# An mLSTM layer with a fused expert block: q and k transposed on the host, scores and state in float32, the output gate in the normaliser

## The chip, the cores and the metric

The kernel runs on one core of one Trainium2 chip. A core has TensorE (matrix products into PSUM), VectorE (DVE), ScalarE (ACT), GpSimd (POOL), and SyncE (SP), which here issues all transfers. The metric is the device time of one launch in microseconds. Three timed runs of the kernel before gave 370.81, 371.1 and 376.52 us; the median is 371.1 us. The change is judged by the same median.

## The reference

For 4 sequences of 768 steps, 8 heads of 40 entries, a gated recurrence gives a row per step; the rows of the heads, side by side, are 3072 rows of 320, and these go through a two-layer block whose middle is a softmax times its own argument, normalised.

```python
m_new = np.maximum(f_gate[:, :, t] + m, i_gate[:, :, t])
f_stab = np.exp(f_gate[:, :, t] + m - m_new)
i_stab = np.exp(i_gate[:, :, t] - m_new)
C = f_stab * C + i_stab * np.einsum('bhd,bhe->bhde', vt, kt)
n = f_stab * n + i_stab * kt
y[:, :, t] = sigmoid(o_gate) * (C q) / np.maximum(np.abs(n q), 1.0)
# then, for all rows x of y:
h = x @ w_in                                   # 320 -> 1024
solu = h * softmax(h)
ln = (solu - mean) / np.sqrt(var + 1e-06) * g_ln
out = ln @ w_out                               # 1024 -> 320
```

The two weights come as float64.

## The kernel before, in words

The 768 steps are cut into 6 chunks of 128, and a *unit* is one chunk of one sequence: 24 units, chunk by chunk, the four sequences in turn. Inside a chunk the recurrence becomes matrix products. A scan over the gates (once, at the start) gives for each step two numbers, kept in `bG`: b, and the exponential of G, the decay since the chunk began. A unit is then:

- Loads: `tk` (v with a column of ones, q and k, row by row), `gb` (G broadcast to all partitions), and every fourth unit `sg` (the output gate for four units, made a sigmoid by ScalarE, L895).
- q and k: the largest entry of each row (`am`, L805), a scale (L819, L824), two float16 parts of each scaled row (`qs`: high parts by ScalarE L828, low parts by VectorE L836), and one transposing transfer to `qT` (L852). In `qT` the 40 entries of a head stand three times, so that one product with 120 rows has high x high, low x high and high x low.
- Decays: GpSimd masks `gb` (L867), ScalarE takes 8 exponentials (`d`, L882). k times the last column of d is `kt` (GpSimd, L904).
- Scores `ps` (8 float16 products, L924); VectorE multiplies them by the decays and the row scale into `p` (L936, two halves).
- y: TensorE multiplies p with v (`sy`, L982, 8 float32 products with 41 columns) and, from the second chunk on, q with the state before (L959, 16 products: the state has three bfloat16 parts, `cs`). VectorE scales the second by exp G (L967), adds the first (L989), and makes the normaliser from column 40 (`rd`: L999, L1008, L1014); x = y times it (L1019), and GpSimd multiplies by the gate (L1031).
- State: 8 products with `kt` as weights (L1045), GpSimd's decay (L1052), VectorE's sum (L1062), and its three bfloat16 parts (L1067, L1071, L1075, L1079), copied to other partitions by two transfers (L1083, L1084).
- x is transposed by TensorE (L1093) and cut into two parts (L1098 to L1110). First product `ph`: 16 products of 512 columns (L1139), in four groups.
- Middle: maximum (L1154), exponential (L1161), e = argument times exponential with its sum (L1169), squares about the mean (L1178). VectorE's small lines L1190 to L1212 collect variance and eps, GpSimd takes powers (L1221), L1229 and L1235 make `so`, the scale of the output rows. GpSimd centres and scales e (`uc`, L1246), ScalarE and GpSimd cut it into two float16 parts (`us`, L1265, L1251), and one transposing transfer gives `big` (L1256).
- Second product `so_`: 24 float16 products of 320 columns (L1283) with two parts of w_out; ScalarE scales them into `ot` (L1299), and a transfer stores them.

At the start the float64 weights are rebuilt as float32 by integer operations on VectorE (L514, L529, L539) and split into parts.

The order of the work is not written by hand. `Plan` records each group with a cost in ns, its reads and writes, and a preference from the table `RANK` (a unit's number plus the entry). `run()` goes through planned time, always gives each engine the best of what it takes to be ready, and issues the groups in that order; each engine keeps it. Groups of TensorE with a `mix` (in the kernel before p times v, and the second product) are issued matrix by matrix in turn where both are ready. Between `bG` and the scale of w_out, `fill` puts products of the identity (L1317) where TensorE would be idle in the plan. PSUM has eight banks: before, `ps` 2, `ph` 2, `sy` 2, `sx` 1 (update of the state, transposes of x), `so_` 1.

Of the kernel before, what the change touches and what calls it, by code (L numbers as in the profile page):

```python
# [20 lines left out]
L = 128  # L21
# [6 lines left out]
HE = H * E1  # L28
NEG = -1.0e30
# [4 lines left out]
SQ = 2.0**8  # L34
SU = 2.0**9
SW = 2.0**14


# var is kept as DFF var, and as var / (DFF SU)^2
EPS_Z = (1.0e-6 * DFF) ** 0.5  # L40
SU_C = 1.0 / (DFF * (DFF * SU) ** 2)

# PSUM buffers: scores, first product, y, small ones, second product
PSB, PHB = 2, 1
BIG = 5
SMALL = {"sy": 2, "sx": 1, "so_": 1}
# [3 lines left out]
RANK = {  # L50
    "sp tk": (12.09, -9.79, -11.5),
    "sp gb": (-1.49, 8.66, 14.2),
    "sp sg": (15.0, -7.54, 1.93),
    "act sg": (-7.1, -1.77, -13.37),
    "dve am": (11.86, -15.0, -0.91),
    "dve rr": (-11.16, -14.0, 13.87),
    "act qs": (0.45, 10.07, 9.68),
    "dve qs": (7.26, 7.15, 10.59),
    "sp qT": (-6.45, 5.48, 11.64),
    "act dec": (-9.23, 5.75, 11.77),  # L60
    "pool gb": (9.8, 13.99, -3.85),
    "act d": (5.39, -8.2, 3.61),
    "pool kt": (8.7, 3.48, -11.6),
    "pe ps": (-9.38, -8.42, 13.4),
    "dve p": (5.27, -1.43, -1.2),
    "pe sy": (0.12, 7.6, -4.18),
    "dve y": (-0.58, -12.54, 10.43),
    "dve rd": (-7.3, -14.52, 10.96),
    "dve x": (-15.0, -11.15, -2.45),
    "pool x": (-5.09, 5.53, 5.17),  # L70
    "pe sx": (-9.5, 2.25, 13.96),
    "pool cn": (8.92, 2.91, 1.53),
    "dve cn": (-2.98, -11.95, -10.92),
# [40 lines left out]
class Plan:  # L114
    """Orders instructions by their costs before any is issued.
# [1247 lines left out]
```

## Time and profile before

| | kernel before |
|---|---|
| timed runs | 370.81, 371.1, 376.52 us, median 371.1 |
| profiled execution, first to last instruction | 374.5 us |
| busy: TensorE, VectorE, ScalarE, GpSimd | 305.6, 323.4, 234.6, 241.9 us |
| mean granted TensorE clock | 0.917 |
| transfers on the hardware queue, share of 16 engines | 73.5% |

The profiled execution is another one than the three timed; its own time is not listed, only its span, so what is worked out from the profile is held against the span and then moved by the 3.4 us between span and median. "Busy" counts the time from an instruction's start to its end, with any wait for a port inside it; "idle before" is time in which an engine had nothing to do, and names what ended it.

### The profile page before, as it was taken

To read this page: it belongs to the slowest core of one execution; us is meant where nothing else is said; L and a number is where in the kernel's file an instruction comes from. 1 tells how busy PE (TensorE), PEld (TensorE's weight loads), DVE (VectorE), ACT (ScalarE), POOL (GpSimd) and SP (SyncE) were. 2 spreads that over 40 slices of the span, in tenths; PEclk is the share of its full clock that TensorE was granted. 3 is DMA by queue.
4 is the path that set the end of the run, shared out by engine and by line. 5 is a ranking of instruction groups with operands and counts; after the bars stand their busy time and mean duration, and the time that the engine had idled before them with its cause. 6 is when DMAs were issued, how large, how long until landed. Compare 5 with 4: busy or idle time off the path is not lost.

```text
span 374.5 us, 7096 instructions
## 1 busy us (share of the span) xinstructions
PE 305.6 (82%) x2469; PEld 251.2 (67%) x2469; DVE 323.4 (86%) x674; ACT 234.6 (63%) x489; POOL 241.9 (65%) x238
## 2 busy tenths in 40 slices
PE   0397969965999797789688885889969899999885
PEld 0397967954788576658566673678748687887653
DVE  8969896989999899999999999889998989865430
ACT  2437743959666667768687664839539879655531
POOL 5476493758696766779864895954866746746500
PEclk9999896988758899989999996969969989999999
DMA  7597989323797969789988897486889867373352
GB/s 224 160 255 219 289 207 279 111 57 96 158 219 193 190 161 184 162 187 235 197 175 153 217 243 164 143 177 136 245 188 205 192 186 166 76 155 74 76 137 63
DMA packets 118724, 65.09 MB, mean 174 GB/s; under 512 B 102880, under 2 KB 110816, under 8 KB 118688
## 3 DMA queue, kind: packets, MB, share of 16 engines
q1 hardware_dynamic: 118688, 64.64, 73.5%
q8 instruction: 19, 0.31, 0.3%
q14 instruction: 17, 0.14, 0.1%
HBM read 33.85 MB, written 4.03 MB: 101 GB/s over the span
## 4 chain that ended last, share of the span: by engine, by line
DVE 49%; PE 37%; issue 6%; DMA 3%; ACT 2%; POOL 1%; SPq 0%; DVEq 0%; ACTq 0%; POOLq 0%
PE ph L1139 14%; DVE qs L836 8%; PE sy L982 4%; DVE p L936 4%; DVE e L1169 4%; DVE nm L1154 4%; DVE so L1229 3%; DMA qT<-qs 3%; DVE am L805 3%; PE sx L1045 2%; DVE rd L1008 2%; DVE so L1235 2%; DVE cs L1075 2%; DVE x L1019 2%; DVE cs L1067 1%
## 5 line engine op out<-in xcount | busy, mean ns | idle before, releaser
L1283 PEld LDWEIGHTS <-big 128*128 128x128 f16 x576 | 64.7, 120 | 22.0 <-issue 6.6
L982 PEld LDWEIGHTS sy<-tk,p 128*128 128x128 f32 x384 | 60.9, 211 | 10.8 <-DVE p L936 8.0
L882 ACT ACTIVATE d<-gb,bG 128x128 f32<-128x128 f32 x192 | 60.0, 390 | 12.0 <-POOL gb L867 12.0
L982 PE MATMUL sy<-tk,p 128*128 128x41 f32 x384 | 59.7, 268 | 7.3 <-DVE p L936 7.3
L1251 POOL TENSOR_TENSOR us<-uc,us 128x1024 f16<-128x1024 f32 x23 | 49.9, 2170 | 14.7 <-ACT us L1265 14.7
L828 ACT ACTIVATE qs<-tk,rr 128x640 f16<-128x640 f32 x48 | 37.8, 822 | 21.1 <-DVE rr L824 15.1
L836 DVE SCALAR_TENSOR_TENSOR qs<-tk,rr,qs 128x320 f16<-128x320 f32 x48 | 44.4, 937 | 0.0
L1139 PE MATMUL ph<-wih,xh 128*128 128x512 f32 x96 | 37.0, 470 | 9.0 <-DVE e L1169 7.8
L1154 DVE TENSOR_REDUCE nm<-ph 128x1 f32<-128x1024 f32 x24 | 29.1, 1215 | 13.5 <-PE ph L1139 13.5
L1161 ACT ACTIVATE e<-ph,nm 128x1024 f32<-128x1024 f32 x24 | 26.6, 1110 | 22.4 <-DVE nm L1154 22.2
L936 DVE SCALAR_TENSOR_TENSOR p<-ps,am,d 128x512 f32<-128x512 f32 x48 | 34.7, 734 | 4.0 <-ACT d L882 2.7
L1178 ACT ACTIVATE sq<-e,nmean 128x1024 bf16<-128x1024 f32 x24 | 27.5, 1144 | 12.3 <-DVE e L1169 12.2
L1031 POOL TENSOR_TENSOR x<-x,sg 128x320 f32<-128x320 f32 x24 | 21.4, 892 | 18.8 <-DVE x L1019 12.4
L1045 PE MATMUL sx<-tk,kt 128*40 128x41 f32 x320 | 18.1, 217 | 18.1 <-DVE x L1110 16.9
L1139 PE MATMUL ph<-wil,xh 128*128 128x512 f32 x96 | 32.6, 423 | 0.0
L1265 ACT CAST us<-uc 128x1024 f16<-128x1024 f32 x24 | 24.9, 1038 | 11.3 <-POOL uc L1246 11.3
L1317 PE MATMUL so__188<-ident 128*128 128x128 f32 x206 | 30.0, 305 | 2.3 <-DVE bG L447 2.3
L1079 POOL TENSOR_TENSOR c<-cr,cs 40x328 bf16<-40x328 f32 x20 | 19.2, 960 | 19.6 <-DVE cs L1075 15.8
L1045 PEld LDWEIGHTS sx<-tk,kt 128*40 128x40 f32 x320 | 15.9, 131 | 22.5 <-issue 20.9
L1317 PEld LDWEIGHTS so__188<-ident 128*128 128x128 f32 x206 | 28.1, 218 | 2.7 <-DVE bG L447 2.5
L1221 POOL TENSOR_TENSOR pw<-ab,mhalf 128x2 f32<-128x2 f32 x24 | 17.3, 719 | 19.2 <-DVE ab L1212 14.7
L1139 PE MATMUL ph<-wih,xl 128*128 128x512 f32 x96 | 29.1, 429 | 0.0
(184 smaller groups left out, 811.0 us busy)
## 6 DMA issues: line engine op xcount, KB each, us to landing
gb<-gd SPq DMA_DIRECT2D x24, 512.0 KB
tk<-in_tok_dram SPq DMA_DIRECT2D x24, 484.0 KB
sg<-in_og_dram SPq DMA_DIRECT2D x12, 320.0 KB
out_dram<-ot SPq DMA_DIRECT2D x24, 160.0 KB
big<-in_w_out_dram SPq DMA_DIRECT2D x4, 640.0 KB
big<-in_w_in_dram SPq DMA_DIRECT2D x4, 512.0 KB
cs<-cs SPq DMA_DIRECT2D x20, 51.2 KB
cs<-c SPq DMA_DIRECT2D x20, 25.6 KB
```

Source lines behind the costliest of these rows:

```text
L828: nc.scalar.activation(out=q_dst(P, a)[:, :, s0 : s1 + 1 : s1 - s0, :], in_=q_src(P, a).unsqueeze(2).to_broadcast([L, H, 2, D]), func=AF.Copy,
L836: V.scalar_tensor_tensor(out=q_dst(P, a)[:, :, 1 + a, :], in0=q_src(P, a), scalar=P[rr][:, a : a + 1], in1=q_dst(P, a)[:, :, 0, :], op0=AL ...
L882: nc.scalar.activation(out=P[d_t][:, h, :], in_=P[gb][:, h, :], func=AF.Exp, bias=P[BG][:, 0, c, b * H + h : b * H + h + 1],)
L936: lambda P, j=j, ps=ps: V.scalar_tensor_tensor(out=P[p_t][:, 4 * j : 4 * j + 4, :], in0=P[ps], scalar=P[am][:, 1:2], in1=P[d_t][:, 4 * j : ...
L982: nc.tensor.matmul(o[:, h, :], lhsT=P[p_t][:, h, :], rhs=v1(P)[:, h, :], start=True, stop=True)
L1045: nc.tensor.matmul(o[:, h, :], lhsT=P[kt][:, h, :], rhs=v1(P)[:, h, :], start=True, stop=True)
L1139: nc.tensor.matmul(P[ph][:, j * 512 : (j + 1) * 512], lhsT=a, rhs=w[:, j * 512 : (j + 1) * 512], start=n == 0, stop=n == 7,)
L1154: lambda P: V.tensor_reduce(out=P[nm], in_=P[ph], axis=AX.X, op=ALU.max, negate=True),
L1178: lambda P: nc.scalar.activation(out=P[sq], in_=P[e], func=AF.Square, bias=P[nmean], scale=-float(DFF), accum_out=P[su]),
L1251: (V if last else nc.gpsimd).tensor_tensor(out=P[us[1]][:, 1], in0=P[uc], in1=P[us[0]][:, 0], op=ALU.subtract)
L1283: nc.tensor.matmul(P[po][:, 0:DM], lhsT=uTv(P, a)[:, k, :], rhs=P[w][:, k, :], start=n == 0, stop=n == 23)
L1317: nc.tensor.matmul(P[("so_", "idle")][:, 0:L], lhsT=P[I], rhs=P[I], start=True, stop=True)
```

## The change

What it does, part by part. Line numbers of the changed kernel's rows are its own.

- **q and k** come from the host transposed (`qkT`): for each unit a tile `qk` of 128 partitions, where the even heads of four pairs lie on partitions 0 to 39 and the odd ones on 64 to 103, zeros elsewhere. `tk` keeps v, the ones and k. Row maxima, scales, float16 parts and their transposing transfer are gone.
- **Scores** are 8 float32 products with 40 rows, a pair's two in turn on the lower and upper rows, into two banks.
- **State** is one float32 tile per sequence, `C`, with the two heads of a pair on the two halves of the partitions; update and use are 4 products each with 82 columns. Its bfloat16 parts and copies are gone. The chunk's decay comes from a small product at the start (`DEC`).
- **y** is summed in PSUM: q times state is scaled by exp G in place, and p times v is added by TensorE on top.
- **Gate**: ScalarE takes exp(-o) in place of the sigmoid; VectorE multiplies 1 + that by the normaliser, takes one reciprocal of 128x320 and multiplies y by it. GpSimd's product with the gate is gone.
- **w_out** is centred once (its column mean, times g, is subtracted), so e goes to float16 as it is, scaled by the row's maximum; GpSimd's `uc` is gone. The scale `so` is made from operations with one tensor operand.
- **PSUM**: `sy` has three banks for scores (two), y, update and transposes of x, taken in a fixed order (`place`); `ph` 2 x 2, `so_` 1.
- **Plan**: groups may carry `lock`; a VectorE group with it and any GpSimd group do not overlap in planned time. An order of issue alone (`issue`) no longer counts as a wait for the end. Costs and the table are new, and the state's two product groups have a `mix` too.
- Some of the start moves: two gate subtractions from GpSimd to VectorE, casts of w_in and the first step of w_out from GpSimd to ScalarE.

Where the order moves, at three places. First TensorE up to its first first product (`so__188`, `so__170`: the filler; `sx`, `sy` with x: transposes of x). Before:

```order
L982 MATMUL sy<-tk,p 128x41 x4
L1317 MATMUL so__188<-ident 128x128 x6
L1093 MATMUL sx<-ident,x 128x128 x2
L1093 MATMUL sx<-ident,x 64x128
L1317 MATMUL so__188<-ident 128x128 x3
L1139 MATMUL ph<-wih,xh 128x512 x2
L1139 MATMUL ph<-wil,xh 128x512 x2
```

On TensorE at the same place, now:

```order
L985 MATMUL sy<-tk,p 128x41 x4
L1051 MATMUL sy<-tk,kt_104 128x82 x4
L1306 MATMUL so__170<-ident 128x128 x15
L1092 MATMUL sy<-ident,x 128x128 x2
L1092 MATMUL sy<-ident,x 64x128
L918 MATMUL sy<-qk 128x128 x8
L1306 MATMUL so__170<-ident 128x128 x2
L1138 MATMUL ph<-wih,xh 128x512 x2
L1138 MATMUL ph<-wil,xh 128x512 x2
```

The next unit's scores now stand ahead of the first product, and those are the last fillers; before, 53 of 103 came after it.

Second, TensorE in a late unit of the changed kernel (`ph` first product, `qk` scores, `big` second product, `C` state):

```order
L1138 MATMUL ph<-wih,xl 128x512 x4
L1092 MATMUL sy<-ident,x 128x128 x2
L1092 MATMUL sy<-ident,x 64x128
L918 MATMUL sy<-qk 128x128 x8
L1138 MATMUL ph<-wih,x_2215 128x512 x2
L1138 MATMUL ph<-wil,x_2215 128x512 x2
L1271 LDWEIGHTS big
L1271 MATMUL so__2377<-woh,big 128x320
L958 MATMUL sy<-C_1243,qk 128x82
L1271 LDWEIGHTS big
L1271 MATMUL so__2377<-wol,big 128x320
L958 MATMUL sy<-C_1243,qk 128x82
```

Before, the 16 products of a unit with the state stood together; now its 4 stand between second products of another unit, and scores stand inside the first product.

Third, VectorE in the middle of the run (`nm` maximum, `qs` float16 parts, `cn` state, `e` the softmax product). Before:

```order
L1154 TENSOR_REDUCE nm<-ph 128x1
L967 TENSOR_TENSOR y<-sy,bG 128x328
L1229 SCALAR_TENSOR_TENSOR so<-ab,pw 128x1
L836 SCALAR_TENSOR_TENSOR qs_86<-tk,rr,qs_86 128x8x40
L1062 TENSOR_TENSOR cn_2210<-cn_2210,sx 40x328
L1235 TENSOR_TENSOR so<-so,ow 128x1
L836 SCALAR_TENSOR_TENSOR qs_86<-tk,rr,qs_86 128x8x40
L1190 TENSOR_SCALAR z<-z 128x1
L1169 SCALAR_TENSOR_TENSOR e,nmean<-ph,e 128x1024
```

On VectorE now, from the maximum to the same product:

```order
L1153 TENSOR_REDUCE nm<-ph 128x1
L931 TENSOR_TENSOR p<-sy,d 128x512
L971 TENSOR_TENSOR sy<-sy,bG 128x328
L1167 TENSOR_SCALAR mx<-nm 128x1
L1168 TENSOR_SCALAR mx<-mx 128x1
L1169 RECIPROCAL s<-mx 128x1
L1078 TENSOR_TENSOR C_1700<-C_1700,sy 64x4x41
L1227 TENSOR_SCALAR z<-z,s 128x1
L1078 TENSOR_TENSOR C_1700<-C_1700,sy 64x4x41
L1236 TENSOR_SCALAR ab<-z 128x1
L1175 SCALAR_TENSOR_TENSOR e,a<-ph,s,e 128x1024
```

The float16 parts of q and k are gone from between; small operations with one tensor operand and the two halves of the state stand there.

The diff, cut to its core:

```diff
 RANK = {
...
+    "pe ps": (-10.92, -4.38, -1.7),
+    "pe yx": (-8.53, 10.05, 2.19),
...
+        self.lock[len(self.ops)] = lock or eng == "pool"
...
-            deps[n].update(first[k] for k in keys)
+            issue[n].update(first[k] for k in keys)
...
+            tiles.sort(key=lambda t: self.place.get(t, 0.0))
...
+                g = max(f, port["pool" if e == "dve" else "dve"])
+                at = {n: max(g if self.lock[n] else f, ready[n]) for n in c}
...
+            if self.lock[n]:
+                port[eng] = end
...
+                for k in (2 * kb, 2 * kb + 1):
+                    nc.tensor.matmul(P[pm][:, 0:DM], lhsT=P[ON], rhs=P[WG][:, k, :], start=k == 0, stop=k == NK - 1)
...
+                lambda P, sl=sl: V.scalar_tensor_tensor(
+                    out=P[WG][:, sl, :],
+                    in0=P[WG][:, sl, :],
+                    scalar=P[sw],
+                    in1=P[WM].unsqueeze(1).to_broadcast([L, 2, DM]),
+                    op0=ALU.mult,
+                    op1=ALU.subtract,
+                ),
...
+        load(1750, lambda P: nc.sync.dma_start(out=P[qk], in_=qkT[b, c]), [qk], prio=rank(SPQ, "qk"), behind=[("gb", u - 2)] if u > 1 else [])
...
+        def score(P):
+            for n in range(NP):
+                for j in range(2):
+                    r = slice(64 * j, 64 * j + D)
+                    nc.tensor.matmul(
+                        P[ps[j]][:, n * L : (n + 1) * L],
+                        lhsT=P[qk][r, 1, n, :],
+                        rhs=P[qk][r, 0, n, :],
+                        start=True,
+                        stop=True,
+                    )
...
+            def inter(P, n):
+                nc.tensor.matmul(
+                    P[yk][:, n * 2 * E1 : (n + 1) * 2 * E1],
+                    lhsT=P[qk][:, 0, n, :],
+                    rhs=P[old][:, n, :],
+                    start=first_of_bank(),
+                    stop=False,
+                    skip_group_check=True,
+                )
...
+            lambda P: V.scalar_tensor_tensor(
+                out=P[rg].rearrange("p (h d) -> p h d", d=D),
+                in0=P[sg][:, u % OG, :].rearrange("p (h d) -> p h d", d=D),
+                scalar=1.0,
+                in1=yv(P)[:, :, D : D + 1].to_broadcast([L, H, D]),
+                op0=ALU.add,
+                op1=ALU.mult,
+            ),
...
+        op(DVE, 420, lambda P: V.reciprocal(out=P[rg], in_=P[rg]), [rg], lock=True)
...
+            def upd(P, n):
+                nc.tensor.matmul(
+                    P[pu][:, n * 2 * E1 : (n + 1) * 2 * E1],
+                    lhsT=P[kt][:, 2 * n : 2 * n + 2, :].rearrange("p a d -> p (a d)"),
+                    rhs=P[tk][:, n * 2 * E1 : (n + 1) * 2 * E1],
+                    start=True,
+                    stop=True,
+                )
...
+        def scale(P):
+            V.tensor_scalar(out=P[mx], in0=P[nm], scalar1=-1.0, scalar2=P[nm], op0=ALU.mult, op1=ALU.max)
+            V.tensor_scalar(out=P[mx], in0=P[mx], scalar1=1.0, scalar2=2.0**-14, op0=ALU.max, op1=ALU.mult)
+            V.reciprocal(out=P[s], in_=P[mx])
...
+        op(ACT, 1040, lambda P: nc.scalar.copy(out=P[us][:, 0], in_=P[e]), [(*us, 0)], [e])
...
+    qkT = np.zeros((B, NC, 2, 64, 2, NP, L), q.dtype)
+    for n, a in enumerate((q, k)):
+        qkT[:, :, :, 0:D, n] = a.reshape(B, NP, 2, NC, L, D).transpose(0, 3, 2, 5, 1, 4)
```

More of the change, by code (lines that the diff above doesn't have):

```diff
@@ L148, in tag, with op @@
         self.tags[name] = (bufs, make)
-    def op(self, eng, ns, fn, out=(), inp=(), prio=0.0, after=0, busy=1.0, behind=(), mix=0):
+    def op(self, eng, ns, fn, out=(), inp=(), prio=0.0, after=0, busy=1.0, behind=(), mix=0, lock=False):
+        self.lock[len(self.ops)] = lock or eng == "pool"
         self.mix[len(self.ops)] = mix
@@ L157, in __getitem__, with needs @@
         return self.tiles[key[:2]]
-    def run(self):
+    def needs(self):
         ops = self.ops
@@ L162, in run @@
         deps = [set() for _ in ops]
+        issue = [set() for _ in ops]
         for n, (_, _, _, out, inp, _, _) in enumerate(ops):
@@ L278, in run @@
         self.span = max(free.values())
+        return order, joint, filled
+    def run(self):
+        ops = self.ops
+        order, joint, filled = self.find()
         skip = set(joint.values())
@@ L441, in tr_gates, with mk_dec @@
             nc.tensor.transpose(pt[:, 1, c, :], gt(P, G_)[:, c * L : (c + 1) * L], P[I][: B * H, : B * H])
-    P.op(PE, 620, tr_gates, [("so_", "g")], [I_, G_, I], prio=g0)
+    P.op(PE, 1100, tr_gates, [PG], [I_, G_, I], prio=g0)
     def mk_bG(P):
-        V.tensor_copy(out=P[BG], in_=P[("so_", "g")].rearrange("p (a c n) -> p a c n", a=2, c=8)[:, :, 0:NC, :])
-    P.op(DVE, 465, mk_bG, [BG], [("so_", "g")], prio=g0)
-    P.op(ACT, 360, lambda P: nc.scalar.activation(out=P[BG][:, 1], in_=P[BG][:, 1], func=AF.Exp), [BG], prio=g0)
+        V.tensor_copy(out=P[BG], in_=P[PG].rearrange("p (a c n) -> p a c n", a=2, c=8)[:, :, 0:NC, :])
+    P.op(DVE, 500, mk_bG, [BG], [PG], prio=g0)
+    P.op(ACT, 430, lambda P: nc.scalar.activation(out=P[BG][:, 1], in_=P[BG][:, 1], func=AF.Exp), [BG], prio=g0)
+    P.op(
+        PE,
+        800,
+        lambda P: nc.tensor.matmul(
+            P[PD][:, 0 : NC * B * H], lhsT=P[SEL], rhs=P[BG][:, 1].rearrange("p c n -> p (c n)"), start=True, stop=True
+        ),
+        [PD],
+        [SEL, BG],
+        prio=g0,
+    )
+    def mk_dec(P):
+        for n in range(2):
+            V.tensor_copy(
+                out=P[DEC][n * 64 : (n + 1) * 64].rearrange("p c b i -> p (c b i)"),
+                in_=P[PD][n * 64 : (n + 1) * 64, 0 : NC * B * H].rearrange("p (n two) -> p n two", two=2)[:, :, n],
+            )
+    P.op(DVE, 500, mk_dec, [DEC], [PD], prio=g0 + 1)
     cst("wih", [L, 3, DFF], F32R)
@@ L673, in scale_w_out @@
             250,
-            lambda P: nc.tensor.matmul(P[pw][:, 256:257], lhsT=P[ON], rhs=P[w1], start=True, stop=True),
+            lambda P: nc.tensor.matmul(P[pw][:, 384:385], lhsT=P[ON][0:1, :], rhs=P[w1], start=True, stop=True),
             [pw],
@@ new lines, in unit, with yv, first_of_bank @@
+        y = [(*yk, j) for j in range(2)]
+        def yv(P):
+            return P[yk][:, 0:HE].rearrange("p (h e) -> p h e", e=E1)
+        begun = []
+        def first_of_bank():
+            begun.append(0)
+            return len(begun) == 1
+        if c > 0:
+            old = Ccur[b]
+            def inter(P, n):
[6 more added lines that the diff above has]
+                    skip_group_check=True,
+                )
+            op(PE, 860, Steps(NP, inter), y, [qk, (*old, 0), (*old, 1)], busy=0.65, mix=1, name="yx")
@@ L1085, in unit @@
-            Ccur[b] = (cn, cs2)
-        px, xh, xl, x3 = (("sx", ("p", u)), ("xh", u), ("xl", u), ("x3", u))
+                    V.tensor_copy(out=P[cn][r, :, w], in_=o)
+            for j in range(2):
+                op(DVE, 300, lambda P, j=j: add_c(P, j), [(*cn, j)], [pu], name="cn")
+            Ccur[b] = cn
+        px, xh, xl, x3 = (bank("p", 0.4), ("xh", u), ("xl", u), ("x3", u))
         def tr_x(P):
```

799 lines of the change are left out of this document (342 added, 457 removed).

## The prediction, made before the result

> **What bounds the kernel now.** I read the page first, then each engine's busy time by stretches, the chain of waits, and then single instructions.
>
> ```profile
> span 374.5 us, 7096 instructions
> ...
> PE 305.6 (82%) x2469; PEld 251.2 (67%) x2469; DVE 323.4 (86%) x674; ACT 234.6 (63%) x489; POOL 241.9 (65%) x238
> ...
> DVE 49%; PE 37%; issue 6%; DMA 3%; ACT 2%; POOL 1%; SPq 0%; DVEq 0%; ACTq 0%; POOLq 0%
> ```
>
> VectorE has the most work and half of the chain. The table by stretches says where (columns: stretch, its length, busy us of PE, PE's weight loads, DVE, ACT, POOL, then PE's granted clock, DMA share, GB/s):
>
> ```profile
> 0.00:40.00 40.00, 22.38 (x173) 21.79 (x174) 34.72 (x47) 17.31 (x33) 23.98 (x31) 0.96 0.80 219
> 80.00:320.00 240.00, 202.10 (x1724) 164.35 (x1724) 226.65 (x491) 169.07 (x362) 170.91 (x162) 0.89 0.81 181
> ```
>
> From 80 to 320 us VectorE works 226.65 of 240 us, 94%. TensorE is busy 84% of that at a clock of 0.89, so it has room. The chain of waits (start, length, instruction) gives the ends of the run:
>
> ```profile
> 39.92 1.86 PE ph L1139 x8
> ...
> 348.62 3.71 PE ph L1139 x16
> ...
> 367.67 3.43 PE so__4616 L1283 x24
> ```
>
> The first of 24 first products starts at 39.9 us, the last at 348.6: 308.7 us for 23 steps, 13.4 us a unit. The last matmul ends at 371.1, 3.4 us before the span does.
>
> Much of VectorE's time is waiting inside an instruction. Per line: minimum, median and longest duration in ns.
>
> ```profile
> L836 DVE SCALAR_TENSOR_TENSOR qs<-tk,rr,qs x48: 495/541/2707, 15.1 to 323.1; 128x320 f16<-128x320 f32 x48
> L1229 DVE SCALAR_TENSOR_TENSOR so<-ab,pw x24: 189/214/4354, 87.5 to 359.5; 128x1 f32<-128x1 f32 x24
> L1190 DVE TENSOR_SCALAR z<-z x24: 90/142/154, 57.2 to 354.9; 128x1 f32<-128x1 f32 x24
> ```
>
> L1229 handles one element a row, and once takes 4354 ns. L1190, as small but with one tensor operand, never exceeds 154. So the long ones do not work longer: they wait, and some kinds of operation never do.
>
> **The change: VectorE.** Groups that go (busy us, mean ns), and one, L1019, that prices what is added:
>
> ```profile
> L836 DVE SCALAR_TENSOR_TENSOR qs<-tk,rr,qs 128x320 f16<-128x320 f32 x48 | 44.4, 937 | 0.0
> L805 DVE TENSOR_REDUCE am<-tk 128x2 f32<-128x640 f32 x24 | 19.3, 803 | 0.0
> L1229 DVE SCALAR_TENSOR_TENSOR so<-ab,pw 128x1 f32<-128x1 f32 x24 | 16.6, 690 | 0.7 <-ACT ot L1299 0.5
> L1235 DVE TENSOR_TENSOR so<-so,ow 128x1 f32<-128x1 f32 x24 | 14.5, 606 | 0.1
> L1019 DVE TENSOR_TENSOR x<-y,rd 128x320 f32<-128x320 f32 x24 | 13.2, 550 | 0.1
> L1008 DVE TENSOR_SCALAR rd<-rd,rr 128x8 f32<-128x8 f32 x24 | 12.8, 532 | 0.1
> L1075 DVE CAST cs<-cr 40x328 bf16<-40x328 f32 x20 | 11.7, 585 | 0.7 <-POOL cr L1071 0.7
> L989 DVE TENSOR_TENSOR y<-y,sy 128x328 f32<-128x328 f32 x20 | 9.7, 487 | 4.7 <-PE sy L982 4.5
> ```
>
> Removed: 44.4 + 19.3 + 16.6 + 14.5 + 12.8 + 11.7 + 9.7 = 129.0 us; smaller groups (the bfloat16 cast of the state, the row maxima's scales) go too and are left as margin. Added per unit: the gate in the normaliser and its reciprocal, 128x320 each, 2 x 0.55 (the reciprocal stays in SBUF; at L836's mean of 0.94 it would be 9 us more in all); about six more small operations at 0.14 to 0.22, say 1.2. That is 2.3 x 24 = 55 us. At the start two gate subtractions and the centring of w_out come over, some 6 us by the 128x320 row. VectorE's new total: 323.4 - 129 + 61 = 255 us at most. Over the forecast time that is 80%: no longer the bound. ScalarE loses the two float16 copies of q and k and all changes between exponential and sigmoid tables; GpSimd loses the centred rows, the gate product and both state differences. Neither was the bound; I cost their edits at nothing. If that cover were gone it would show as a wait in the ring below.
>
> **The change: TensorE.** Full-clock prices, from one engine's timeline; a group's price is the distance from its start to the next group's. (A float32 matmul shows as two records: x16 is 8 matmuls.)
>
> ```profile
> 29.21 2.25 PE L1317 MATMUL so__188<-ident 128*128 128x128 f32 x18
> 31.30 0.61 PE L924 MATMUL ps<-qT 120*128 120x128 f16 x8
> ...
> 115.69 0.98 PE L982 MATMUL sy<-tk,p 128*128 128x41 f32 x8
> 116.50 0.31 PE L1283 MATMUL so__1235<-woh,big 128*128 128x320 f16 x1
> ...
> 122.50 0.81 PE L1045 MATMUL sx<-tk,kt 128*40 128x41 f32 x16
> 123.24 0.74 PE L1139 MATMUL ph<-wih,xh 128*128 128x512 f32 x2
> ...
> 304.17 0.61 PE L924 MATMUL ps<-qT 120*128 120x128 f16 x8
> 304.62 0.56 PE L959 MATMUL sy<-cs,qT 120*128 120x41 bf16 x16
> 305.03 0.71 PE L1139 MATMUL ph<-wih,xh 128*128 128x512 f32 x2
> ...
> 308.80 0.31 PE L1283 MATMUL so__3899<-woh,big 128*128 128x320 f16 x1
> 308.95 0.31 PE L982 MATMUL sy<-tk,p 128*128 128x41 f32 x2
> 309.09 0.31 PE L1283 MATMUL so__3899<-wol,big 128*128 128x320 f16 x1
> ...
> 310.22 0.49 PE L1093 MATMUL sx<-ident,x 128*128 128x128 f32 x3
> 310.55 0.30 PE L1283 MATMUL so__3899<-woh,big 128*128 128x320 f16 x1
> ```
>
> Unchanged per unit: first product 308.80 - 305.03 = 3.77 us, second product 3.43 (the chain's row), transposes of x 0.33.
> - Scores: now 0.45 us in float16. Eight float32 128x128 matmuls, each like the filler's (2.09 us for 9, 0.232): 1.86 us if one follows another, 0.93 if the two of a pair, in different rows of the array, run together. No row shows such a pair. I take the middle, 1.4, and keep both ends.
> - Scores times v: 0.14 each where it stands between second-product matmuls, 0.81 / 4 = 0.20 alone. By the new order 124 of 192 are mixed: 31.2 us in all (before 128 mixed, 30.7).
> - State into y, and update of the state: 160 float32 matmuls with 82 columns instead of 320 16-bit and 160 float32 ones. Between the mixed 41-column price, 0.14, and the 128-column one, 0.232; I take 0.19, 30.4 us in all (before 20 x (0.41 + 0.74) = 23.0).
> - Mean of w_out: 8 matmuls of 320 columns, 2.5 x 0.232 = 0.58 each, 4.6 us.
>
> Sum: 24 x (3.77 + 3.43 + 0.33 + 1.4) = 214.3; + 31.2 + 30.4 + 4.6 = 280.5 us. The same sum for the kernel before is 24 x (3.77 + 3.43 + 0.33 + 0.45) + 30.7 + 23.0 = 245. So the change gives TensorE 35 us more to do; it pays because VectorE's bound lay above both. What is late next is TensorE.
>
> On the pairs the Trainium skill gives two rules. "TensorE: Matmul & The Clock Gate", Part 3, has matmuls in different row groups run concurrently, which would be the 0.93 end, 11 us less in all. "TensorEngine Tiling", Key Properties, has every change of tiling mode drain the array, which speaks against this change; no run here shows either yet.
>
> **Start, queues and end.** Ahead of the first first product VectorE now has three L805 at 0.80 and four L836 at 0.54 for the first units, 4.6 us that go; its share of 0 to 40 us is 34.72, so it is what the start waits for. First product at 39.9 - 4.6 = 35.3 if all of it counts, 39.9 if none; I take 36. The new order has 46 fillers ahead of it and none later (103 before, half of them later). On SP a unit's issue of the q and k transpose goes and one plain load comes:
>
> ```profile
> L852 SPq DMA_TRANSPOSE qT<-qs x24: 1605/2005/6052, 16.5 to 324.2; - x24
> ```
>
> That is 2.0 us of SP a unit, and a chain from VectorE through the transfer to the scores, both gone. Two small copies of the state a unit go as well. The load of 512 KB has no producer on the core, so it can be early. I cost it at nothing; it is covered by three buffers, and without that cover a unit would wait for it as it now does for the transpose.
>
> Before its first product at 36 us TensorE has done two scores, one unit's scores times v, one update, one transpose: 5.5 us. Left: 275 us. As the bound VectorE ran at 94%; TensorE after the last first product, with a backlog, at nearly 100% and full clock. Between these I take 97%: 283.5. Sum: 36 + 283.5 + 3.4 (last matmul to the end of the span) = 322.9 in the profiled execution. That one spans 374.5, the median of the three timed runs is 371.1; less 3.4 us: 319.5. I write 318.
>
> **Rivals.**
> - *Faster still.* Pairs together and no gaps: 36 + 275 - 11.3 = 300 us. For it: in the new order the pairs alternate between the two halves of the array. Against: nothing yet ran at 100% for a whole run.
> - *The array drains at each change between half and whole.* Two changes a unit. A second-product record lasts 0.31 us and the next begins 0.15 after it: about 0.16 to wait, 48 x 0.16 = 8 us, 326. For it: scores stand between full-array groups in every unit. It is the rule of "TensorEngine Tiling" in the Trainium skill, named above; against it only that no run here has shown it.
> - *The ring of three banks.* Scores, y, update and transposes now share three buffers in a fixed order: a unit's scores take the banks that the last unit's y and update held. Scores 1.4, decays 2 x 0.73, scores times v 1.6, normaliser to x 2.05: 6.5 us; and each step queues behind long work.
>
> ```profile
> L936 DVE SCALAR_TENSOR_TENSOR p<-ps,am,d 128x512 f32<-128x512 f32 x48 | 34.7, 734 | 4.0 <-ACT d L882 2.7
> L1154 DVE TENSOR_REDUCE nm<-ph 128x1 f32<-128x1024 f32 x24 | 29.1, 1215 | 13.5 <-PE ph L1139 13.5
> ```
>
> Three visits to VectorE behind a 1.2 us reduction and two to TensorE behind a quarter of a first product (0.94) make 12.0 us, above TensorE's 275 / 24 = 11.5. At 12.5 a unit: 36 + 300 = 336. At 13.8 nothing would be gained.
> - *The stalls stay.* If the nine small VectorE operations of a unit stalled to L1229's mean of 690 instead of about 200, 9 x 0.49 x 24 = 106 us would come back: VectorE 361, at 94% and with the 22 us after the last reduction 404. It decides from 0.34 us each. For it: L1008, with one tensor operand but eight columns, has a mean of 532. Against: seven of the nine are one column wide with one tensor operand, like L1190, and the two with eight columns work on PSUM.
> - *Slower by the clock.* The granted clock falls where TensorE has gaps:
>
> ```profile
> 80.00:120.00 40.00, 34.34 (x252) 28.62 (x252) 37.02 (x86) 27.69 (x60) 28.97 (x30) 0.74 0.74 160
> ```
>
> At 0.74 throughout, 275 / 0.74 = 372, and 36 more: 408 us, slower than before. It decides from a clock of 275 / 335 = 0.82. Against: in the last stretch, where TensorE had a backlog, the clock was full, and the change makes it the one with a backlog.
>
> **Chances.** Forecast (303 to 333 us) 0.51, drains 0.10, faster still 0.14, ring 0.18, no gain (ring at 13.8) 0.02, stalls 0.02, clock 0.03. Score price 0.93 to 1.86 moves the sum by 11 us each way, 94 or 100% by 8, the start by 4: the range 299 to 342 takes these in with most of the ring, and leaves out the upper ends. 2% is 7.4 us, about what a measurement can tell: faster 0.94, within 0.02, slower 0.04.
>
> **What would show it.** TensorE over 93% busy from 40 us on at a clock near 1.0, VectorE near 80%, no small VectorE operation with a maximum above 1 us; scores at 0.9 to 1.9 us a unit; first first product near 36 us and the last some 11.5 x 23 later. It is wrong if TensorE waits on VectorE's x or decay lines in every unit (ring), if its clock stays near 0.9, or if VectorE is still above 90%.

## Result: 351.1 us, faster by 5%, less than half of the forecast gain

Four executions of the changed kernel took 350.09 to 353.96 us, median 351.09; the kernel before, on the same chip, had a median of 370.96. The ratio is 0.949, interval [0.944, 0.953]. The forecast was 318, and its range ended at 342.

The page of the changed kernel (profiled in the execution of 353.96 us):

```profile
span 352.2 us, 6325 instructions
...
PE 307.8 (87%) x2245; PEld 254.1 (72%) x2245; DVE 263.6 (75%) x565; ACT 186.4 (53%) x421; POOL 139.8 (40%) x143
...
PE 63%; DVE 31%; issue 3%; DMA 2%; ACT 1%; SPq 0%; ACTq 0%; DVEq 0%
DVE rg L1031 14%; PE ph L1138 13%; PE sy L985 8%; PE sy L918 7%; PE sy L958 5%; PE sy L1051 4%; PE sy L1092 3%; PE so__170 L1306 3%; DVE x L1035 3%; DVE rg L1020 3%; DVE e L1175 1%; DVE nm L1153 1%; PE so__3547 L1271 1%; PE so__3781 L1271 1%; PE so__1488 L1271 1%
```

VectorE's busy time fell from 323.4 to 263.6 us and its share of the chain from 49 to 31%. But the largest single entry of the chain, 14%, is now an instruction that the change added, the reciprocal of the gate. Its row (minimum, median, longest in ns):

```profile
L1031 DVE RECIPROCAL rg<-rg x24: 2139/2153/2154, 31.0 to 329.0; 128x320 f32<-128x320 f32 x24
```

It takes 2.15 us, the same each time, so it works and does not wait. The forecast had it at 0.55. VectorE's timeline shows what stands between two of them (start, length, instruction, idle time before it and what ended that):

```profile
173.02 2.15 DVE L1031 RECIPROCAL rg<-rg 128x320 f32<-128x320 f32 x1
175.21 0.49 DVE L1035 TENSOR_TENSOR x<-sy,rg 128x320 f32<-128x320 f32 x1
...
177.72 0.69 DVE L931 TENSOR_TENSOR p<-sy,d 128x512 f32<-128x512 f32 x1
178.63 1.23 DVE L1153 TENSOR_REDUCE nm<-ph 128x1 f32<-128x1024 f32 x1 [0.23 <-PE ph L1138]
180.06 0.51 DVE L971 TENSOR_TENSOR sy<-sy,bG 128x328 f32<-128x328 f32 x1 [0.20 <-PE sy L958]
180.47 0.68 DVE L931 TENSOR_TENSOR p<-sy,d 128x512 f32<-128x512 f32 x1
...
184.43 0.17 DVE L1001 TENSOR_SCALAR na<-sy 128x8 f32<-128x8 f32 x1 [0.47 <-PE sy L985]
...
185.36 2.15 DVE L1031 RECIPROCAL rg<-rg 128x320 f32<-128x320 f32 x1
```

and TensorE's timeline the part of the same turn that lies there:

```profile
173.89 1.09 PE L1138 MATMUL ph<-wih,xl 128*128 128x512 f32 x4
175.85 0.52 PE L1092 MATMUL sy<-ident,x 128*128 128x128 f32 x3 [0.87 <-DVE ab L1243]
176.30 1.16 PE L918 MATMUL sy<-qk 40*128 40x128 f32 x16
177.39 0.74 PE L1138 MATMUL ph<-wih,x 128*128 128x512 f32 x2
```

Read together they are one ring: reciprocal, x, transposes of x (L1092), the next unit's scores (L918) in the same three banks, their decays (L931, the second half behind the maximum L1153 and the scaling of y, L971), p times v on TensorE until 184.4, normaliser, gate, reciprocal again: 185.36 - 173.02 = 12.34 us. The next reciprocal starts at 197.69. TensorE, with some 11.4 us of work in a turn, sits idle for 0.87 us of it ahead of the transposes. (The profile names L1243 as what ended that idle time; it is the instruction behind x on VectorE, and x itself ends at 175.70.) Over the run, from the list of TensorE's waits:

```profile
PE sy L1092 <- DVE x L1035: 11.8, 9, 3.1
...
PE sy L1092 <- DVE ab L1243: 8.8, 10, 0.9
PE sy L1092 <- DVE z L1227: 3.2, 2, 2.6
```

(columns: us in total, times, longest). Nearly 24 us in 21 waits, for 24 units, always at the transposes of x.

### The profile page after: what moved, and what is told of

It reads as the page before. It is cut to its first block, busy times and chain, and to the rows that moved or that the text cites. A ratio compares the mean times of both kernels' runs of the same rounds, so it can differ in the third digit from the quotient of the medians.

```text
span 352.2 us, 6325 instructions
## 1 busy us (share of the span) xinstructions
PE 307.8 (87%) x2245; PEld 254.1 (72%) x2245; DVE 263.6 (75%) x565; ACT 186.4 (53%) x421; POOL 139.8 (40%) x143
## 4 chain that ended last, share of the span: by engine, by line
PE 63%; DVE 31%; issue 3%; DMA 2%; ACT 1%; SPq 0%; ACTq 0%; DVEq 0%
DVE rg L1031 14%; PE ph L1138 13%; PE sy L985 8%; PE sy L918 7%; PE sy L958 5%; PE sy L1051 4%; PE sy L1092 3%; PE so__170 L1306 3%; DVE x L1035 3%; DVE rg L1020 3%; DVE e L1175 1%; DVE nm L1153 1%; PE so__3547 L1271 1%; PE so__3781 L1271 1%; PE so__1488 L1271 1%
## 5 line engine op out<-in xcount | busy, mean ns | idle before, releaser
L873 ACT ACTIVATE d<-gb,bG 128x128 f32<-128x128 f32 x192 | 59.1, 390 | 10.7 <-DVE p L931 7.5
L1203 POOL TENSOR_TENSOR us<-e,us 128x1024 f16<-128x1024 f32 x23 | 49.1, 2138 | 17.8 <-issue 12.3
L1031 DVE RECIPROCAL rg<-rg 128x320 f32<-128x320 f32 x24 | 51.6, 2151 | 0.6
L931 DVE TENSOR_TENSOR p<-sy,d 128x512 f32<-128x512 f32 x48 | 31.9, 685 | 6.6 <-ACT d L873 4.0
L1092 PE MATMUL sy<-ident,x 128*128 128x128 f32 (+1 forms) x72 | 12.5, 282 | 24.1 <-DVE x L1035 11.8
L1175 DVE SCALAR_TENSOR_TENSOR e<-ph,s,e 128x1024 f32<-128x1024 f32 x24 | 30.7, 1280 | 0.9 <-ACT e L1160 0.7
L1153 DVE TENSOR_REDUCE nm<-ph 128x1 f32<-128x1024 f32 x24 | 29.3, 1220 | 2.8 <-PE ph L1138 2.7
L1092 PEld LDWEIGHTS sy<-ident,x 128*128 128x128 f32 (+1 forms) x72 | 6.7, 131 | 33.4 <-issue 28.6
L858 POOL TENSOR_SCALAR_AFFINE_SELECT gb<-gb 128x1024 f32<-128x1024 f32 x24 | 26.9, 1121 | 7.0 <-DMA gb<-gd 7.0
L958 PEld LDWEIGHTS sy<-C,qk 128*128 128x128 f32 x160 | 27.6, 212 | 2.7 <-PE so__965 L1271 1.1
L1185 ACT ACTIVATE sq<-e,a 128x1024 bf16<-128x1024 f32 x24 | 27.4, 1142 | 3.1 <-DVE e L1175 3.0
L918 PE MATMUL sy<-qk 40*128 40x128 f32 x384 | 28.8, 291 | 0.0
L958 PE MATMUL sy<-C,qk 128*128 128x82 f32 x160 | 28.2, 279 | 0.7 <-DVE x L1109 0.6
L918 PEld LDWEIGHTS sy<-qk 40*128 40x128 f32 x384 | 24.1, 193 | 5.0 <-PE sy L1092 4.0
```

The costliest lines, as they stand in the source:

```text
L873: nc.scalar.activation(out=P[d_t][:, j, n, :], in_=P[gb][:, h, :], func=AF.Exp, bias=P[BG][:, 0, c, b * H + h : b * H + h + 1],)
L918: nc.tensor.matmul(P[ps[j]][:, n * L : (n + 1) * L], lhsT=P[qk][r, 1, n, :], rhs=P[qk][r, 0, n, :], start=True, stop=True,)
L931: lambda P, j=j: V.tensor_tensor(out=P[p_t][:, j], in0=P[ps[j]].rearrange("p (n l) -> p n l", l=L), in1=P[d_t][:, j], op=ALU.mult,),
L958: nc.tensor.matmul(P[yk][:, n * 2 * E1 : (n + 1) * 2 * E1], lhsT=P[qk][:, 0, n, :], rhs=P[old][:, n, :], start=first_of_bank(), stop=False ...
L1031: op(DVE, 420, lambda P: V.reciprocal(out=P[rg], in_=P[rg]), [rg], lock=True)
L1092: nc.tensor.transpose(P[px][0:w, k * L : (k + 1) * L], P[x][:, k * L : k * L + w], P[I])
```

## Experiments

Two theories stood against each other at first: the reciprocal is on a ring that sets the period (theory 1), or it lies beside other work and something else, TensorE's queue or the planner's order, sets it. All kernels below are made from the changed one; except where it is said, every instruction keeps its place in every engine's queue. (The expectations number theories and rivals as they came up; theory 4, which comes in with the wide reciprocal behind x, is not the rival 4 of the planner's cost.) Times are medians; levels of the kernel before differed a little between the groups of runs (371.0, 373.9 and 371.5 us), so the ratios are what to compare.

**A narrow reciprocal.**

```diff
-  activation(out=P[sg], in_=P[sg], func=AF.Exp, scale=-1.0)
+  activation(out=P[sg], in_=P[sg], func=AF.Tanh, scale=0.5)
-  na: scalar1=-WS, scalar2=WS;  next line: scalar=WS
+  na: scalar1=-2.0 * WS, scalar2=2.0 * WS;  next line: scalar=2.0 * WS
+  V.reciprocal(out=yv(P)[:, :, D], in_=yv(P)[:, :, D])          # 128x8
   scalar_tensor_tensor(out=rg, in0=sg, scalar=1.0, in1=yv[:, :, D], add, mult)
-  V.reciprocal(out=P[rg], in_=P[rg])                            # 128x320
```

> The gate becomes 0.5 * (1 + tanh(o/2)), so the factor 2 goes into the normaliser, the reciprocal is taken of the 8 normalisers (128x8) before the gate multiply instead of the 128x320 product behind it, and every instruction keeps its place in every queue. Only the reciprocal's 2.15 us (its row in the changed kernel) becomes about 0.2 us (the row of the 128x8 reciprocal of the kernel before, 0.19). Theory 1, the reciprocal lies on the ring that hands the banks of scores, y and x from unit to unit, and the ring sets the period of 12.33 us: the ring shrinks to 12.33 - 1.96 = 10.4, TensorE's own work of 11.46 per unit takes over, 0.87 x 24 = 21 us less, more where units took over 12.5: 326 to 332 us. Rival 2, the reciprocal lies beside other work and TensorE's in-order queue sets the period with the gaps merely showing up there: 347 to 352. Rival 3, the ring binds but another wait of it comes next (the banks' other users, a queue order found for a reciprocal of 0.42 us): 336 to 345.

Measured: 325.47 us, ratio 0.880 [0.872, 0.889]. Theory 1, and a little more than it asked for. Against the kernel as changed, this one edit is worth 25.6 us. ScalarE's tanh costs what its exponential did (7.5 and 7.6 us in all, L887), so the gain is not from there. The same stretch of TensorE's timeline:

```profile
178.74 1.08 PE L1142 MATMUL ph<-wih,xl 128*128 128x512 f32 x4
179.66 0.49 PE L1096 MATMUL sy<-ident,x 128*128 128x128 f32 x3
180.08 1.16 PE L918 MATMUL sy<-qk 40*128 40x128 f32 x16
181.17 0.73 PE L1142 MATMUL ph<-wih,x 128*128 128x512 f32 x2
```

In the regular part no idle time is left ahead of the transposes, and the period is 11.27 us. This is the fastest kernel of the study, together with the last one below.

**The reciprocal twice.**

```diff
+  V.reciprocal(out=P[x], in_=P[rg])
   V.reciprocal(out=P[rg], in_=P[rg])
```

> The changed kernel with its 128x320 reciprocal issued twice in a row, the first into x, which the multiply then overwrites; the order of every queue is otherwise kept. VectorE has 24 x 2.15 = 52 us more, and is idle for 88 us of the span now. Theory 1, the reciprocal is on the ring that sets the period: all of it is added, 351 + 24 x 2.15 = 403 us (395 to 407). Rival 2, it lies beside other work: less than a third of it, 351 to 368.

Measured: 445.33 and 453.37 us in two executions, so at least 94 more than the changed kernel where theory 1 said 52. That it is on the ring is not in doubt, but it costs nearly twice its length. The profile is of the longer one (mean granted clock 0.849, the other 0.861). From the windows (stretch, its length, busy us of the engines, granted clock, DMA share, GB/s) and from TensorE's timeline in the same kernel:

```profile
160.00:200.00 40.00, 34.65 (x215) 28.59 (x214) 27.91 (x60) 17.99 (x45) 12.92 (x12) 0.79 0.52 144
```

```profile
190.43 0.87 PE L1096 MATMUL sy<-ident,x 128*128 128x128 f32 x3 [3.14 <-DVE x L1039]
191.23 2.08 PE L918 MATMUL sy<-qk 40*128 40x128 f32 x16
```

With 3.14 us of idle time ahead, the transposes take 0.87 us in place of 0.52 and the scores 2.08 in place of 1.16, and the granted clock is 0.79 from 160 to 200 us in place of 1.00. These slow products are themselves on the ring. The Trainium skill ("TensorE: Matmul & The Clock Gate", Part 1) has a clock that is either whole or half, set by how busy the array was in a free-running window of about 3.4 us; the records here grow by 1.7 and 1.8 times, which does not speak against it. That the lower clock is all of the difference between 52 and 94 us was not separated.

**The planner's cost of the reciprocal.**

```diff
-  op(DVE, 420, ... V.reciprocal ...)
+  op(DVE, 2150, ... V.reciprocal ...)
```

> The changed kernel with one number of its planner changed: the reciprocal is costed at 2150 instead of 420, so that the order of all queues is found for the reciprocal as it is. No instruction is added or taken away. Theory 1, the ring (scores, decays, yi, normaliser, reciprocal, x, px) sets the period whatever stands between: 345 to 353 us. Rival 4, the order is at fault and with the true cost the planner finds other matmuls for the gap ahead of px: 326 to 338.

Measured: 397.83 us, ratio 1.079 [1.071, 1.088]: neither case. With the true cost the planner found an order 13% slower than with the wrong one. VectorE in a unit of it:

```profile
217.34 0.49 DVE L1020 SCALAR_TENSOR_TENSOR rg<-sg,sy 128x320 f32<-128x320 f32 x1
218.91 1.22 DVE L1153 TENSOR_REDUCE nm<-ph 128x1 f32<-128x1024 f32 x1 [1.09 <-PE ph L1138]
...
220.69 2.13 DVE L1031 RECIPROCAL rg<-rg 128x320 f32<-128x320 f32 x1
...
222.86 0.49 DVE L1035 TENSOR_TENSOR x<-sy,rg 128x320 f32<-128x320 f32 x1
```

and TensorE:

```profile
223.50 0.52 PE L1092 MATMUL sy<-ident,x 128*128 128x128 f32 x3 [4.62 <-DVE x L1035]
223.94 2.08 PE L918 MATMUL sy<-qk 40*128 40x128 f32 x16
```

In this unit the new order puts the maximum L1153 and three small operations between the gate and its reciprocal. The maximum waits 1.09 us for the first product to end, the reciprocal waits in the queue behind it, and TensorE is idle for 4.62 us and then runs at the lower clock. From unit 9 on, the starts of x lie some 14 and some 16.5 us apart in turn. Why the planner, which knows all waits, chose this was not followed further.

**Scores without pairs.**

```diff
-  for n in range(NP):
-      for j in range(2):
+  for j in range(2):
+      for n in range(NP):
```

> The eight score products of a unit are issued as four of the even heads and then four of the odd ones, instead of in pairs of an even and an odd head that use different halves of the array's rows. Nothing else moves. If a pair's two products run side by side, the 1.09 us per unit becomes up to 1.86 us (eight times 0.23), and as the scores stand on the ring the time grows by up to 24 x 0.77 = 18 us, to 365 to 371. If pairing does nothing, 351. If the scores grow but do not stand on the ring, 351 to 355 with the scores' rows at 1.8 us.

Measured: 378.22 us, 27 more than the changed kernel. TensorE's timeline, in a turn at full clock and in one in which the clock fell:

```profile
174.43 1.71 PE L918 MATMUL sy<-qk 40*128 40x128 f32 x16
176.07 0.73 PE L1138 MATMUL ph<-wih,x 128*128 128x512 f32 x2
...
190.72 0.56 PE L958 MATMUL sy<-C,qk 128*128 128x82 f32 x2
```

A unit's scores last 1.64 us from their start to the next group's, in place of 177.39 - 176.30 = 1.09: running in pairs saves a third, not half. On the ring this gives 12.33 + 0.55 = 12.88, which is the length of the shorter periods; but from unit 11 on about every second one is 14.5, with the state's products (L958) at 0.56 us where they take 0.35 in the other turns. In such a turn the granted clock was 0.72 from 188 to 194 us, and 1.00 from 194 to 214; the same fall comes five times up to 303 us, two turns apart, though no idle time of TensorE from 150 to 310 us is longer than 0.9 us. Five such turns add 5 x 1.6 = 8 of the 14 us that the longer scores alone (24 x 0.55 = 13) do not explain; the other 6 were not followed, and what sets the clock's fall in every second turn is not shown.

**How much of the reciprocal fits beside TensorE.** With the narrow kernel as a base, half of the wide reciprocal at its old place:

```diff
+  V.reciprocal(out=P[x][:, 0 : DM // 2], in_=P[rg][:, 0 : DM // 2])   # between gate and x
```

> The kernel with the narrow reciprocal in the same order, and at the place of the wide one, between the gate multiply and x, a reciprocal of 128x160 into x, which the multiply then overwrites. By the slope between the 128x8 row (0.22) and the 128x320 row (2.15) it takes 1.15 us. Theory 1, a ring of 10.4 us beside TensorE's 11.5 per unit: the ring grows to about 11.5 and just reaches TensorE's work, so that little is lost: 326 to 334 us. Rival, every microsecond between the gate and x costs 24 of them whatever TensorE has to do: 325.5 + 24 x 1.15 = 353, or half of the way between 325.5 and 351.1, 338, if the cost is in proportion.

Measured: 331.75 us, ratio 0.888 [0.882, 0.895], 3 us more than the narrow kernel by the ratios. It took 1.15 us, as expected:

```profile
L1035 DVE RECIPROCAL x<-rg x24: 1143/1153/1155, 30.8 to 307.6; 128x160 f32<-128x160 f32 x24
```

With 0.04 us from one instruction to the next, the ring without it is 12.33 - 2.19 + 0.25 = 10.39 us (the 0.25 is the 128x8 reciprocal), and with it 10.39 + 1.19 = 11.58. The regular period of this kernel is 11.58. In the regular part the first half of the reciprocal's cost is almost free (0.31 us of 1.19), since TensorE needs 11.27 anyway. The second half is paid in full: with a reciprocal of 128x320 at this place in the units from 9 on (below) the period is 12.59, and 10.39 + 2.19 = 12.58.

**The wide reciprocal behind x.** The same work for VectorE at another place:

```diff
   V.tensor_tensor(out=x, in0=yv[:, :, 0:D], in1=rg, op=ALU.mult)
+  V.reciprocal(out=P[rg], in_=P[rg])
```

> The kernel with the narrow reciprocal in the same order, and behind the multiply that makes x a 128x320 reciprocal of the gate into itself, which nobody reads any more. VectorE has as much work as in the changed kernel (0.2 us more per unit), but the 2.15 us lie behind x, in the time in which TensorE transposes x and forms the next scores (0.45 + 1.09 us) and which VectorE spent mostly idle in the narrow kernel's timeline. If the place on the ring made the reciprocal dear: 325 to 332 us. If it was VectorE's load: 345 to 352, as in the changed kernel.

Measured: 344.59 us, ratio 0.920 [0.916, 0.925]: between the two. The windows of the changed, the narrow and this kernel, in this order (stretch, its length, busy us of PE, PE's weight loads, DVE, ACT, POOL, PE's granted clock, DMA share, GB/s):

```profile
40.00:80.00 40.00, 34.45 (x218) 27.79 (x216) 36.03 (x79) 25.83 (x67) 24.66 (x27) 0.96 0.65 188
80.00:120.00 40.00, 35.42 (x235) 29.29 (x236) 27.73 (x62) 22.55 (x51) 18.97 (x19) 0.83 0.56 145
160.00:200.00 40.00, 37.04 (x285) 30.78 (x283) 33.30 (x70) 22.82 (x52) 15.59 (x15) 1.00 0.73 188
```

```profile
40.00:80.00 40.00, 39.23 (x268) 32.10 (x266) 37.03 (x89) 31.69 (x78) 28.75 (x28) 1.00 0.83 225
80.00:120.00 40.00, 35.00 (x287) 29.56 (x287) 27.58 (x78) 25.48 (x60) 21.14 (x22) 1.00 0.51 144
160.00:200.00 40.00, 40.00 (x330) 34.94 (x330) 29.72 (x80) 24.89 (x60) 17.77 (x18) 1.00 0.77 196
```

```profile
40.00:80.00 40.00, 36.12 (x205) 29.45 (x204) 35.04 (x76) 25.84 (x67) 21.10 (x25) 0.87 0.59 174
80.00:120.00 40.00, 32.88 (x215) 25.80 (x214) 31.22 (x66) 20.86 (x46) 22.36 (x20) 0.87 0.60 149
160.00:200.00 40.00, 40.00 (x319) 34.29 (x320) 35.18 (x79) 25.36 (x59) 17.06 (x17) 1.00 0.75 191
```

From 160 us on the third kernel is as good as the second: TensorE busy without a gap at full clock, though VectorE has 35.18 us of work in 40. Before 120 us it is no better than the first. So there are two stages. In the early one VectorE still prepares the weights, and in the narrow kernel it is 37.03 of 40 us busy between 40 and 80 us. A further theory, called theory 4 below: in this stage every microsecond on VectorE counts, wherever it stands; behind it only those on the ring do.

**The two stages apart.** The narrow kernel with the wide reciprocal on the ring in units 0 to 8 only, in units 9 to 23 only, and behind x in units 0 to 8 only:

```diff
+  if u < 9:  V.reciprocal(out=P[x], in_=P[rg])     # between gate and x (second kernel: u >= 9)
   ...
+  if u < 9:  V.reciprocal(out=P[rg], in_=P[rg])    # third kernel: behind the multiply that makes x
```

> The narrow kernel in the same order, with a 128x320 reciprocal between the gate multiply and x (into x, which the multiply then overwrites) in units 0 to 8 only, while VectorE still prepares the weights. From the starts of x in the two profiles: x of unit 9 starts at 150.5 us in the changed kernel and at 133.1 in the narrow one. If that stage holds a loss of its own, all of it (17 us) is carried to the end: 325.5 + 14 to 18 = 339 to 344, a ratio to before of 0.915 to 0.925. If only the regular part behind it decides, and this stage catches up while the queues are deep: 325 to 331, below 0.895.

> The same with the 128x320 reciprocal in units 9 to 23 only. Ring against TensorE: the period becomes 12.33 in place of 11.27 there, 11 x 1.06 = 12 us up to unit 20 and 4 in the last three: 325.5 + 16 = 341.5, 338 to 344, a ratio of 0.915 to 0.925. If the early stage alone set the difference: 325 to 331, below 0.895.

> The narrow kernel in the same order, with a 128x320 reciprocal behind x, which nobody reads, in units 0 to 8 only. Theory 4, the early stage is bound by VectorE itself (37 of 40 us busy from 40 to 80 us in the narrow kernel), where every microsecond on it counts wherever it stands, and behind that stage the place behind x is free: all of the loss of the kernel with it in every unit is here, 341 to 346, a ratio of 0.912 to 0.925. Rival, the loss was spread over all units by the place in VectorE's queue: a third to a half of it, 331 to 336, 0.890 to 0.905.

Measured: 339.71 us, ratio 0.914 [0.907, 0.921]; 345.97 us, 0.925 [0.914, 0.935]; 340.31 us, 0.915 [0.909, 0.921]. All three fit theory 4: the first time is inside its range, the third 1 us below, the second 2 us above (its four executions took 341.37 to 347.02 us), and the ratios are inside theirs or 0.001 off. From the starts of x on VectorE's timeline in each profile, the time between units (us):

| kernel | unit 0 to 9 | 9 to 20 | 20 to 23 |
|---|---|---|---|
| changed | 117.3 | 135.7 | 45.2 |
| narrow | 102.0 | 123.8 | 41.1 |
| half on the ring | 108.0 | 127.4 | 41.6 |
| wide behind x, all units | 120.7 | 125.2 | 41.6 |
| wide on the ring, units 0 to 8 | 118.3 | 123.8 | 41.1 |
| wide on the ring, units 9 to 23 | 108.0 | 138.4 | 46.9 |
| wide behind x, units 0 to 8 | 121.0 | 123.8 | 41.1 |

In the regular part, from unit 9 to 20, the reciprocal costs 12 to 15 us on the ring and 1.4 behind x. In the early stage it costs 15 to 19 us by these profiles, on the ring and off it, against 9 x 2.15 = 19 of its own. Not all of that is VectorE's time. The granted clock lay between 0.83 and 0.96 in both stretches, 40 to 80 and 80 to 120 us, of the four kernels with the early reciprocal, and was 1.00 in the narrow kernel's profile. That profile was of its fastest execution, 321.66 us at a mean clock of 1.0; the other three had 0.979 to 0.984 and took 325 to 326. By the medians, which level most of this out, the reciprocals of units 0 to 8 cost 14 us on the ring and 15 behind x (12 and 13 by the ratios), two thirds to three quarters of their own time.

So it is shown that in this stage the place does not matter and most of the length is paid. That a full VectorE is the reason is argued from its busy time, not shown alone: it is busy for 33 to 37 of 40 us from 40 to 80 us in these kernels, but only 28 to 32 from 80 to 120, and what the lower clock adds there was not separated.

Two notes on the sixth row. It is from the longest of that kernel's four executions. And of its 6 us before unit 9, 2.2 are the reciprocal of unit 9, which stands ahead of that unit's x; nearly all of the rest comes between the x of units 5 and 6 (14.1 us, 10.7 in the narrow kernel), where the instructions are those of the narrow kernel and the granted clock was 0.56 from 90 to 100 us against 1.00. One such fall of the clock is worth some 3.4 us here, and the differences between rows of that column hold up to that much of chance.

**The planner without the port.**

```diff
-  self.lock[len(self.ops)] = lock or eng == "pool"
+  self.lock[len(self.ops)] = False
```

> The changed kernel with the planner's knowledge of the shared port taken out: no instruction is held until the other engine's has ended, and the order of all queues is found anew; the instructions are the same. If that knowledge is what removed the stalls of the small VectorE operations (470 to 690 ns on average in the kernel before, about 200 now), they come back to 300 to 600 ns in their rows, some 1 us per unit, and the time to 355 to 375 us. If the stalls went with the work that left GpSimd (242 to 140 us busy), the rows stay near 200 ns, and the time moves only by the order, 345 to 357.

Measured: 348.19 us, ratio 0.932 [0.927, 0.936], no slower than the changed kernel. The row of the scale `so` in the changed kernel, and in this one (busy us, mean ns, idle before):

```profile
L1257 DVE TENSOR_SCALAR so<-pw,ow 128x1 f32<-128x1 f32 x24 | 5.0, 209 | 9.3 <-POOL pw L1250 9.1 <-ACT ot L1287 0.3
```

```profile
L1257 DVE TENSOR_SCALAR so<-pw,ow 128x1 f32<-128x1 f32 x24 | 4.9, 210 | 8.9 <-POOL pw L1250 8.8
```

The stalls that reached 4354 ns in the kernel before (its L1229) did not come back: the longest of this row is 216 ns. So they did not go because the planner knows the port. Whether they went with the form of the operations (one tensor operand) or with GpSimd's lighter load (241.9 to 139.8 us) was not separated.

**The order found anew for the narrow reciprocal.**

```diff
+  op(DVE, 190, ... V.reciprocal of 128x8 ...)       # ahead of the gate, own cost
```

> The narrow reciprocal with its own cost of 190 in the planner, ahead of the gate multiply, so that the order of all queues is found anew. If TensorE's 11.5 us per unit is the bound, no order of the rest can do much better: 320 to 328 us; but an order that puts other VectorE work ahead of the gate, as the one found with the cost of 2150 did, would be slower, 330 to 345.

Measured: 328.72 us, 0.7 above the first range; the ratio, 0.880 [0.876, 0.885], is the same as with the old order. From 120 to 240 us TensorE is busy without a gap in both, so an order of the same work can gain nothing there.

## Why the prediction was wrong

**The step that failed** is "the gate in the normaliser and its reciprocal, 128x320 each, 2 x 0.55": a reciprocal was priced by a multiply of the same shape (L1019). The gate multiply was right (L1020, 483 ns). The reciprocal measured 2.15 us, beyond even the 0.94 that was given as the worst case. The trace of before held its price. Per line, minimum, median and longest:

```profile
L824 DVE RECIPROCAL rr<-am x24: 143/154/167, 13.6 to 311.6; 128x2 f32<-128x2 f32 x24
```

```profile
L1014 DVE RECIPROCAL rd<-rd x24: 180/190/203, 33.1 to 340.3; 128x8 f32<-128x8 f32 x24
```

Six more columns cost 36 ns, 6 ns a column; 312 more would be 1.87 us, 2.06 in all. Two rows of the right operation at two widths were worth more than one row of the right shape. The runs give (2153 - 1153) / 160 = 6.25 ns a column. The Trainium skill says ("VectorE: DVE Perf Modes", under the fixed hardware budget) that the reciprocal is an iterative divide with a repeat count of 8; it gives no duration, but it speaks against the price of a multiply. On that the rows agree, with 2.15 us against 0.49; the count itself no row here shows.

**What followed from it.** The ring was the rival with a chance of 0.18 and 336 us. It took place, at 12.33 us a unit against the 12.0 to 12.5 worked out for it. That agreement is partly luck: without the reciprocal the measured ring is 12.33 - 2.15 = 10.2, and the lower end of the one worked out 12.0 - 0.55 = 11.45, so the rest of the ring, most of it queueing, had been put 1.3 too high and the reciprocal 1.6 too low. What the rival lacked altogether was the early stage, where the reciprocal is paid for off the ring too: 15 of the 31 us by which the profiles of the changed and the narrow kernel differ from the first x to the last, with the clock's part in it. So it gave 336 where 351 was measured.

**A second term that was off** is the last step, "less 3.4 us", from the span to the time. It set the profiled span, 374.5, against the median of other executions. In every execution of which both are on record, the time is 1.7 to 2.2 us longer than the span; by that the profiled execution took some 376.5 itself and was a long one. A span of 322.9 is then a time of some 324.7, not 319.5; and the 318 that was written is 1.5 lower again, with no term for it. Together that is 6.7 us of the miss of 33; the reciprocal is 25.6 of it by the narrow kernel, whose median of 325.47 is close to the 324.7.

**Right.** The other terms of the sum, as the narrow kernel shows, where only the reciprocal's size differs. Forecast span 322.9; its four executions have 319.9 to 324.3. First first product at 36 us: 35.85 in the changed kernel. TensorE's work a unit: 275 / 24 = 11.46 forecast, 11.27 in the narrow kernel's regular part. That 97% came out for the whole is in part luck: TensorE was busy 54.23 of 60 us from 40 to 100 us, and without a gap at a clock of 1.00 from 120 to 240; and after the last first product starts, 19 us of the last unit follow, which the sum had not shown apart. Scores: 1.4 taken, 1.09 measured, inside the stated ends.

VectorE's total, "255 us at most", did not hold: 263.6 measured, since the reciprocal alone is 24 x 1.6 = 38 us above its price. The other terms left a margin, as the 222.9 with the narrow reciprocal show.

**The other rivals.** The array's drain at each change of tiling, the rule of "TensorEngine Tiling" in the Trainium skill: in the narrow kernel scores and transposes stand between whole-array products with no idle time, and the period of 11.27 is not above the sum of a unit's products, 3.77 + 3.43 + 0.33 + 1.09 + 1.30 + 1.52 = 11.44, so no cost of it shows here. A small one is not excluded: it could lie inside the scores' 1.09, or in the 0.42 us from the transposes' start to the scores', where the row before had 0.33. Faster still: the pairs run side by side only in part, and TensorE's regular part is free of gaps only where the wide reciprocal is off the ring. Stalls: none; the small VectorE operations of a unit never exceed 216 ns. The clock: it was 0.83 between 80 and 120 us, but 0.97 over the changed kernel's run.

## What to carry to other kernels

Price an operation by rows of the same operation, at two widths if there are two, and only then by its shape; for a new instruction on a path that closes from unit to unit, work out the ring and the bound beside it with both prices. An edit that takes 2 us from such a ring is worth only what the ring has above the next bound (12.33 to 11.27 here), but in a stage in which the engine itself is nearly full it was worth most of it, wherever it stood. A wait that empties TensorE costs more than its length when the clock falls after it. And turn a span into a time by an execution of which both are known.

## What was not expected of the hardware

- A reciprocal of 320 columns takes 2.15 us where a multiply of the same shape takes 0.49; its slope is 6.2 ns a column from 8 to 320 columns.
- Eight float32 score products of 40 rows take 1.09 us when those of a pair alternate between the two halves of the rows and 1.64 when they do not.
- In the kernel with the reciprocal twice, TensorE waited some 3 us a unit for x, the granted clock was 0.79 in the stretch from 160 to 200 us, and the 52 us added cost at least 94.
- With the scores not in pairs, the clock fell in every second turn though no gap of TensorE was longer than 0.9 us; in the changed kernel, with gaps of 0.87 us, it stayed at 1.00 from 160 to 200 us.
